# Keys of a gated linear attention turned head by head in half of the array's rows, two units ahead, with f and k loaded a step sooner

## The chip, the cores and the metric

The kernel runs on one core of a Trainium2 chip. The metric is the device time of one execution in microseconds. The engines are named as in the profile: PE (TensorE, matrix products; PEld is its weight load), DVE (VectorE), ACT (ScalarE), POOL (GpSimd) and SP (SyncE, which here issues transfers).

## What is computed

Two parts, one behind the other, all in FP32: a recurrence with a state per head, and a bilinear feed-forward layer.

```python
# q, k, v, f_logit: (4, 8, 768, 48); w_a, w_b: (384, 1536); w_out: (1536, 384)
f = 1.0 / (1.0 + np.exp(-f_logit))
for t in range(S):
    state = f[:, :, t, :, None] * state + np.einsum('bhd,bhe->bhde', k[:, :, t], v[:, :, t])
    y[:, :, t] = np.einsum('bhd,bhde->bhe', q[:, :, t], state)
x = y.transpose(0, 2, 1, 3).reshape(B * S, H * D)      # 3072 x 384
return ((x @ w_a) * (x @ w_b)) @ w_out
```

## The kernel before, in words

**Units and blocks.** The recurrence is cut into 16 units: a batch, half of its tokens (384) and four heads. In a unit's tiles two heads lie one above the other, in rows 0 to 47 and 64 to 111, and two such pairs side by side (`n`). Tokens go in chunks of 128 (`c`) and sub-chunks of 64 (`p`). Two units fill a block: 384 tokens of x with all 384 columns. There are eight blocks.

**The steps of a unit** (all in `by_quotients`):
- `loads_of` (line 209): transfers of f, k, q (two each, one for each half of the rows) and v on the SP queue, into one of three sets of tiles, so that a unit's loads wait until the unit three before has done with them.
- `front_parts` (line 302): ACT makes sigmoid(f) and its opposite, POOL an affine step; DVE scans f (L322), takes reciprocals (L330), scans the inverse (six of L335), multiplies k by the inverse and q by the products of f (L339).
- `scores` (L392): 24 products of k with q, 64 tokens each, in quarters of the array, into the bank pair ps_x.
- `mask` (L405): DVE reads ps_x and writes the masked scores to `at`.
- `turn` (L416): six transposes of 128 x 128, each of one chunk of one pair of heads, all 128 rows at once, into ps_x, over the scores that the mask has read. `turned` (L425) copies them to kT on ACT.
- `gains` (L440): products of kT and v for each sub-chunk, into ps_x over the transposes; `carry` (L467, L469) adds them to the states on DVE, and `hand_on` (L478) scales the last state for the other half of the tokens.
- `within` (L489) and `across` (L515): products of `at` with v and of the states with q, both into ps_y; `out_of_bank` (L534) copies ps_y out with three copies on ACT, and `stores_of` (L554) moves it into the block's xT with five small transfers on SP.

**The layer.** Blocks 0 and 1 go through plain products (`up`, L598; `product`, L620 on DVE). For blocks 2 to 7 `up_triples` (from line 714, products at L720) computes both factors with 15 products in place of 18; it works on sums of weights (`combine_w_ba`, L633 and, where DVE makes them, L1262) and of x (`combine_x`, L704), in four quarters `j` of 15 steps each. ACT copies (L1307 through a planner's line) and DVE adds (L712) take the results out of four banks, ps_f. `down` (products at L822) multiplies by w_out for pairs of token groups, with seven products in place of eight; DVE and ACT add up (L837 to L857), and SP stores rows of the result (L861).

**What sets the order of work.** The first four units and the first products are written out by hand. From there on a list `main` holds the layer's steps, and a planner (line 1168 on) lays the remaining work between them: `Line` objects hold steps with an engine, a planned cost and marks that they need, and `fill` emits the first step of any line that fits: for PE when its inputs are planned to be there, for other engines when `delays` finds that no step of `main` would come late by it. `emit_until` forces what a block must have before it starts. There are six lines, tried in this order:

```python
for_out, for_x, core, fore, loads, for_ba = lines = [Line() for _ in range(6)]
```

`core` holds `core_parts(s)` (line 901) for s = 4 to 16, strictly in order: within of unit s-1 and scores of s; mask; turn; turned; gains of s and across of s-1; carries; hand-on; copies out and stores of s-1. `fore` holds the fronts, `loads` the transfers of unit s, which wait for the stores of unit s-3. A unit's scores wait for its whole front. PE visits a unit three times: within and scores, turn, gains and across.

Of the kernel before, what the change touches and what calls it, by code (L numbers as in the profile page):

```python
# [12 lines left out]
FP32 = mybir.dt.float32  # L13
# [7 lines left out]
C = 128  # L21
FINE = (0, 1, 2, 4, 8, 16)
BLK = 384
# [3 lines left out]
R = 64  # L27
# [115 lines left out]
def by_quotients(ctx, tc, q, k, f_logit, v, moe_w_a, moe_w_b, moe_w_out, out, ident, weights, bad, ps_f):  # L143
    nc = tc.nc
    B, H, D, S = q.shape
# [4 lines left out]
    NQ = H // 4  # L150
    NC = BLK // C
# [3 lines left out]
    NU = B * NH * NQ  # L155
    NBLK = B * NH
    NSET = 3
# [3 lines left out]
    sb1 = ctx.enter_context(tc.tile_pool(name="sb1", bufs=1))  # L161
# [8 lines left out]
    sets = []  # L170
    for i in range(NSET):
        t = {n: fixed([128, 2, BLK], f"{n}_in{i}") for n in "qkf"}
# [120 lines left out]
    PE, DVE, ACT, POOL, SP = range(5)  # L293
    live = {}
# [4 lines left out]
    def halves(x):  # L299
        return x.rearrange("p n s -> p (n s)")  # L300
# [55 lines left out]
    ps_x, ps_y = (ps_a.tile([128, 2, 512], FP32, tag=n, name=n) for n in ("ps_x", "ps_y"))  # L356
# [23 lines left out]
    def pair_of(x):  # L380

        return [x[:, i] for i in range(2)]
# [17 lines left out]
    def mask(u):  # L400
# [4 lines left out]
        nc.vector.tensor_tensor(to, x, tri.broadcast_to((128, 2, 2 * NC, SUB)), ALU.mult)  # L405
        live[u]["at"] = at

    def turn(u):

        kf = halves(sets[u % NSET]["k"])  # L410
        live.setdefault(u, {})["kT"] = sb1.tile([128, 2, NC, 128], FP32, tag="kT", name="kT")
        ps = live[u]["turned"] = [ps_f[idle.pop(0)] for _ in range(2)] if u in FIRST else pair_of(away(u))
        for n in range(2):
            for c in range(NC):
                o = n * BLK + c * C
                nc.tensor.transpose(ps[n][:, c * C:c * C + C], kf[:, o:o + C], ident)  # L416
# [10 lines left out]
    def gains(u, chunks=range(NC)):  # L427

        _, half, _ = unit(u)
        t, kT = sets[u % NSET], live[u]["kT"]  # L430
        last = half == NH - 1
        ps = live[u]["turned"]
        for n in range(2):
            for c in chunks:
                for p in range(2):
                    if last and c == NC - 1 and p == 1:
                        continue
                    for h in range(2):
                        r = slice(SUB * p, SUB * p + SUB)
                        nc.tensor.matmul(  # L440
                            ps[p][R * h:R * h + D, (n * NC + c) * D:(n * NC + c) * D + D],
                            lhsT=kT[r, n, c, R * h:R * h + D],
                            rhs=t["v"][r, n, c, h * D:h * D + D],
                            start=True,
                            stop=True,
                        )
# [126 lines left out]
    ISSUE = 430  # L573
# [327 lines left out]
    def core_parts(s):  # L901


        u = s - 1
        if u < 2 * NQ:
            yield PE, 1000, 0, scores, s
        elif s < NU:
            yield PE, 1600, 0, within_and_scores, u
        else:
            yield PE, 1000, 20 * BEAT, within, u  # L910
        if s < NU:
            yield DVE, 880, 0, mask, s
            yield PE, 850, 0, turn, s
            yield ACT, 700, 0, turned, s
        if u < 2 * NQ:
            yield PE, 1000, 0, gains, s
        elif s < NU:
            yield PE, 1550, 0, gains_and_across, u
        else:
            yield PE, 1000, 0, across, u  # L920
        if s < NU:
            for j in range(NJ - 1 if unit(s)[1] == NH - 1 else NJ):
                yield DVE, 180, 0, carry, s, j
            if unit(s)[1] < NH - 1:
                yield DVE, 320, 0, hand_on, s
        if u >= 2 * NQ:
            for part in range(3):
                yield ACT, 490, 0, out_of_bank, u, part
            begin, *stores = stores_of(u)
            yield SP, 0, 0, begin  # L930
            for do in stores:
                yield SP, ISSUE, 5000, do

    def within_and_scores(u):
        within(u)
# [1 line left out]

    def gains_and_across(u):
        gains(u + 1)
        across(u)  # L940

    some = fixed([128, 2], "some")

# [30 lines left out]
    with tc.manual_schedule():  # L974
# [161 lines left out]


        w_out_sums, (w_before, w_over) = list(combine_w_out()), combine_w_ba()
        main, beside, behind, ending = [], {}, {}, []
        for blk, i in ups[alone:]:  # L1140
            main.extend(up_steps(blk, i))
            main.append(on(DVE, 480, 2, product))
# [2 lines left out]
        for blk in range(NBLK):  # L1145
            if blk >= 2:
                beside[len(main)] = "x", blk
                main.extend(up_triples(blk))
                behind[blk] = len(main)
                ahead = 16  # L1150
            b, odd = divmod(blk, 2)
            pairs = (((blk - 1, 0), (blk, 0)), ((blk, 1), (blk, 2))) if odd else (((blk, 1), (blk, 2)),)
            if blk == 1:
                pairs = (((0, 1), (0, 2)), *pairs)
            for two in pairs if blk else ():
                beside.setdefault(len(main), "out")
                first, *steps = down(two, ending if blk == NBLK - 1 and two is pairs[-1] else None)
                at = len(main) - ahead
                main.insert(at, first)
                beside = {n + (n > at): x for n, x in beside.items()}  # L1160
                if blk == NBLK - 1 and two is pairs[0]:
                    steps.insert(0, on(DVE, 700, 0, sum_held))
                    steps.append(on(PE, 100, 0, check_held))
                main.extend(steps)
                behind.setdefault("down", len(main))
                ahead = 10
# [11 lines left out]
                    needs, past = (), 0  # L1178
                return self, len(self.steps)

        for_out, for_x, core, fore, loads, for_ba = lines = [Line() for _ in range(6)]
        marks = {"out": for_out.extend(w_out_sums)}
        for_ba.extend(w_before)
        marks["ba"] = for_ba.extend(w_over, past=behind[1])
        stores = {}
        for s in range(2 * NQ, NU + 1):
            if s < NU:
                loaded = ()
                if s - NSET in stores:
                    at = stores[s - NSET]  # L1190
                    loaded = (loads.extend([(SP, ISSUE, 6000, do) for do in loads_of(s)], needs=(at,)),)
                ready = fore.extend(
                    [(e, load, 0, *do) for part in front_parts(s) for e, load, *do in part], needs=loaded
                )
            for step in core_parts(s):
                blk, second = divmod(s - 1, NQ)
                core.extend(
                    (step,),
                    needs=(ready,) if step[3] in (scores, within_and_scores) else (),
                    past=behind[blk - 2] if step[3] in (across, gains_and_across) and not second else 0,  # L1200
                )
            if s > 2 * NQ:
                stores[s - 1] = core, len(core.steps)
# [88 lines left out]
        for done, (engine, load, due, do, *args) in enumerate(main):  # L1292
# [8 lines left out]
            else:  # L1301
                ready = max(now, last_copy if engine >= COPIED else 0) + LATENCY
# [357 lines left out]
```

## Time and profile before

| | us |
|---|---|
| median of 3 runs | 597.28 (597.1 to 597.85) |
| the profiled execution: its own time | 596.37 |
| its span | 594.6 |
| DVE, ACT, POOL busy | 412.2, 268.7, 77.7 |
| PE idle after 130 us of the span, in all | 2.3 |

What the stages are, by the time in the span: up to 50 us loads, first units and the conversion of the first weights; 50 to 139 plain products of blocks 0 and 1; 139 to 192 the first down phases; from 192 on block after block (2 to 7) a product phase and a down phase. Units 4 to 15 pass through between 128 and 467 us. The last two blocks have no attention work beside them.

Some groups by shape, for the steps that the change concerns (columns: line, engine, operation, names, shapes, count; busy us, mean ns; idle before):

```profile
L416 PE MATMUL ps_x<-ident,k_in 128*128 128x128 f32 x78 | 10.6, 273 | 0.0
L440 PE MATMUL ps_x<-v_in,kT 64*48 64x48 f32 x568 | 10.0, 209 | 0.5 <-issue 0.5
L425 ACT COPY kT<-ps_x 128x768 f32<-128x768 f32 x13 | 10.4, 798 | 44.5 <-PE ps_x L416 43.7 <-DVE sums L712 0.8
```

A matmul's mean is its length from first input to last output; matmuls follow one another at shorter distance, so their cost to the stream is read from start to start. An FP32 product stands in the trace as two records, a transpose as one. The page counts PE as idle only where no matmul is in flight, so short stops between records don't show as idle.

### The profile page before, as it was taken

How to read it: one execution, taken by the hardware profiler on the slowest of the kernel's cores; microseconds unless marked ns; L12 is line 12 of the kernel's file. 1: busy time of each engine (PE TensorE's matmuls, PEld its weight loads, DVE VectorE, ACT ScalarE, POOL GpSimd, SP SyncE). 2: the span in 40 equal slices, each digit the busy share in tenths (PEclk: the TensorE clock that was granted, in tenths of full speed). 3: DMA queues.
4: the chain of work that ended last, by engine and by line, in shares of the span. 5: the costliest groups of instructions: out<-in, count | busy, mean ns of one | idle time of the engine just before them, and what ended most of it. 6: DMA issues, size and time to landing. Idle time of an engine off the chain costs nothing.

```text
span 594.6 us, 13952 instructions
## 1 busy us (share of the span) xinstructions
PE 572.6 (96%) x5802; PEld 512.9 (86%) x5802; DVE 412.2 (69%) x786; ACT 268.7 (45%) x507; POOL 77.7 (13%) x71
## 2 busy tenths in 40 slices
PE   2899999999999999999999999999999999999997
PEld 1655655557999999999999999999999999999996
DVE  6899545599978678958894678847785165836751
ACT  6589959753132464245521444326431345135300
POOL 6254425355000000000000000000000000000000
PEclk9899999999999999999999999999999999999999
DMA  9696699089542440044004410041001100000001
GB/s 211 183 267 197 213 273 268 0 147 186 116 141 71 115 93 10 15 120 95 2 1 125 108 23 2 2 105 43 3 1 47 48 1 0 2 28 1 0 29 33
DMA packets 33561, 49.43 MB, mean 83 GB/s; under 512 B 3984, under 2 KB 25264, under 8 KB 33488
## 3 DMA queue, kind: packets, MB, share of 16 engines
q1 hardware_dynamic: 30000, 42.19, 25.5%
q0 software_dynamic: 3056, 5.92, 5.9%
q8 instruction: 47, 0.77, 0.5%
q10 hardware_dynamic: 432, 0.34, 0.2%
q14 instruction: 26, 0.21, 0.1%
HBM read 33.23 MB, written 4.72 MB: 64 GB/s over the span
## 4 chain that ended last, share of the span: by engine, by line
PE 85%; DVE 10%; issue 2%; ACT 1%; DMA 1%; SPq 0%; DVEq 0%; ACTq 0%
PE ps_f L720 35%; PE ps_f L822 28%; PE ps_f L598 13%; PE ps_y L489 2%; DVE inv L335 2%; PE ps_y L515 2%; PE ps_x L392 2%; PE ps_x L440 1%; PE ps_x L416 1%; DVE sums L712 1%; DVE groups L712 1%; DVE spare L335 1%; DVE q_in L339 1%; DVE f_in L322 1%; DVE w_ba L73 1%
## 5 line engine op out<-in xcount | busy, mean ns | idle before, releaser
L598 PE MATMUL ps_f<-xT,w_ba 128*128 128x384 f32 x288 | 95.6, 489 | 1.5 <-DMA xT<-y 1.4
L1307 ACT COPY sums<-ps_f 128x384 f32<-128x384 f32 x120 | 57.4, 480 | 75.9 <-PE ps_f L720 68.2
L598 PEld LDWEIGHTS ps_f<-xT,w_ba 128*128 128x128 f32 x288 | 53.8, 190 | 38.2 <-issue 2.2
L1307 ACT COPY groups<-ps_f 128x384 f32<-128x384 f32 x120 | 57.7, 481 | 62.9 <-PE ps_f L720 39.9
L720 PE MATMUL ps_f<-xT,w_ba 128*128 128x192 f32 x384 | 78.4, 327 | 0.0
L720 PEld LDWEIGHTS ps_f<-xT,w_ba 128*128 128x128 f32 x384 | 64.7, 190 | 0.2
L720 PE MATMUL ps_f<-groups,w_ba 128*128 128x192 f32 x288 | 55.5, 327 | 0.0
L720 PE MATMUL ps_f<-x_sums,raw 128*128 128x192 f32 x288 | 54.1, 331 | 1.2 <-DVE groups L712 0.9
L822 PE MATMUL ps_f<-w_out,sums 128*128 128x192 f32 x288 | 52.2, 329 | 0.3 <-DVE groups L620 0.3
L822 PE MATMUL ps_f<-w_out,groups 128*128 128x192 f32 x288 | 51.7, 328 | 0.0
L720 PEld LDWEIGHTS ps_f<-x_sums,raw 128*128 128x128 f32 x288 | 46.9, 190 | 4.3 <-DVE groups L712 1.8
L822 PE MATMUL ps_f<-spare,sums 128*128 128x192 f32 x288 | 49.0, 326 | 0.0
L720 PEld LDWEIGHTS ps_f<-groups,w_ba 128*128 128x128 f32 x288 | 47.8, 190 | 0.5 <-ACT groups L1307 0.3
L822 PEld LDWEIGHTS ps_f<-w_out,sums 128*128 128x128 f32 x288 | 47.1, 190 | 1.3 <-DVE groups L620 0.6
L318 POOL TENSOR_SCALAR inv<-inv 128x768 f32<-128x768 f32 x14 | 13.1, 935 | 266.7 <-ACT inv L315 266.7
L822 PEld LDWEIGHTS ps_f<-w_out,groups 128*128 128x128 f32 x288 | 47.1, 190 | 0.7
L822 PEld LDWEIGHTS ps_f<-spare,sums 128*128 128x128 f32 x288 | 47.1, 190 | 0.1
L60 POOL TENSOR_SCALAR sums<-sums 128x768 f32<-128x768 f32 (+1 forms) x20 | 40.4, 2018 | 43.9 <-ACT sums L58 43.8
L712 DVE TENSOR_TENSOR sums<-sums,groups 128x768 f32<-128x768 f32 x36 | 34.7, 965 | 14.2 <-ACT groups L1307 13.7
L712 DVE TENSOR_TENSOR sums<-ps_f,sums 128x384 f32<-128x384 f32 x60 | 32.8, 553 | 16.5 <-PE ps_f L720 15.0
L720 PE MATMUL ps_f<-x_sums,w_ba 128*128 128x192 f32 x192 | 39.3, 327 | 0.5 <-DVE sums L712 0.5
L720 PE MATMUL ps_f<-xT,raw 128*128 128x192 f32 x192 | 39.4, 328 | 0.0
(142 smaller groups left out, 869.3 us busy)
## 6 DMA issues: line engine op xcount, KB each, us to landing
raw<-w_ba POOLq DMA_DIRECT2D x11, 512.0 KB, 8.6
k_in<-in_k_dram SPq DMA_DIRECT2D x32, 144.0 KB, 4.2
q_in<-in_q_dram SPq DMA_DIRECT2D x32, 144.0 KB, 4.4
v_in<-in_v_dram SPq DMA_DIRECT2D x16, 288.0 KB, 5.0
raw<-in_moe_w_out_dram SPq DMA_DIRECT2D x6, 768.0 KB, 5.9
out_dram<-o SPq DMA_DIRECT2D x22, 192.0 KB, 1.9
f_in<-in_f_logit_dram SPq DMA_DIRECT2D x28, 144.0 KB, 3.0
xT<-y SPq DMA_DIRECT2D x45, 72.0 KB, 2.2
```

Source lines behind the costliest of these rows:

```text
L60: nc.gpsimd.tensor_scalar(h, h, HI_MAX, None, ALU.min)
L73: nc.vector.tensor_tensor(dst[:, rows], hu[:, rows], bit[:, rows], ALU.add)
L318: nc.gpsimd.tensor_scalar(inv, inv, EXP_K, 1.0, ALU.mult, ALU.add)
L335: nc.vector.tensor_tensor_scan(inv[:, w], inv[:, w], none[:, 0:C], first, ALU.mult, ALU.add)
L392: nc.tensor.matmul(ps[h][SUB * p:SUB * p + SUB, o:o + SUB], lhsT=kf[r, tokens(n, c, p)], rhs=qf[r, tokens(n, c, p)], start=True, stop=True,)
L489: nc.tensor.matmul(ps[p][e:e + D, o:o + SUB], lhsT=t["v"][r, n, c, h * D:h * D + D], rhs=at[r, h, o:o + SUB], start=o == 0, stop=True, ski ...
L515: nc.tensor.matmul(ps[p][e:e + D, o:o + SUB], lhsT=st[j][r, n], rhs=qf[r, tokens(n, c, p)], start=False, stop=True, skip_group_check=True,)
L598: nc.tensor.matmul(ps[nm][:, 0:BLK], lhsT=w[:, kt, ft * 128:ft * 128 + 128], rhs=xT[blk][:, kt], start=kt == 0, stop=kt == NKT - 1,)
L712: nc.vector.tensor_tensor(to, x, y, op)
L720: nc.tensor.matmul(ps[:, g], lhsT=sums_of_w[name][:, g, 128 * j:128 * j + 128], rhs=sums_of_x[blk][name], start=start and g == 0, stop=Tru ...
L822: nc.tensor.matmul(to, lhsT=x[:, i // 2, i % 2], rhs=w[:, NI * (i % 2) + i // 2], start=start and i == 0, stop=i == HFT - 1, skip_group_ch ...
L1307: do(*args)
```

## The change

- `turn` is kept for units 0 to 3. From unit 4 on `turn_heads` makes twelve transposes in place of six: for each chunk and pair, the upper and the lower head by itself, 48 rows in, 48 columns out, into bank h of a pair.
- From unit 8 (`AHEAD`) on these transposes stand in the step of `gains_and_across` two units earlier, behind `across`. They go to columns of ps_x behind the gains (four chunks) and of ps_y behind the outputs (two chunks), and `turned_heads` copies them with two copies of 384 and 192 columns. For units 4 to 7 they stay where `turn` stood, and one copy of 576 columns takes them out.
- kT lies head by head, 48 columns each without gaps; `gains` reads it through `keys`.
- Copies out, stores, the q product of the front, and the last sums of w_b and w_a get lines of their own. The front without its q product waits for f and k, and gains (from unit 8 on) wait for it; scores wait for the q product.
- f and k of a unit are loaded when unit s-3 has handed its state on; q and v as before behind its stores.

The order of instructions that results: 72 transposes of 128 columns are replaced by 144 of 48, thirteen copies to kT of 768 columns by one of 768, four of 576, and eight each of 384 and 192; on DVE, POOL and SP the same instructions stand in another order.

```diff
+    AHEAD = 4 * NQ
+    NX = 4
+    turns = [(n * NC + c, n, c) for n in range(2) for c in range(NC)]
+    def turn_heads(u):
+        kf = halves(sets[u % NSET]["k"])
...
+        live[u]["turned"] = pair_of(ps_x)
+        for i, n, c in turns:
+            ps, o = (ps_x, 2 * NC * D + i * D) if i < NX else (ps_y, BLK + (i - NX) * D)
+            if u < AHEAD:
+                ps, o = ps_x, i * D
+            for h in range(2):
+                r, at = slice(R * h, R * h + D), n * BLK + c * C
+                nc.tensor.transpose(ps[:, h, o:o + D], kf[r, at:at + C], ident[r, R * h:R * h + D])
...
+        if u < AHEAD:
+            copy(0, ps_x, 0)
+        else:
+            copy(0, ps_x, 2 * NC * D)
+            copy(NX, ps_y, BLK)
...
-                            lhsT=kT[r, n, c, R * h:R * h + D],
+                            lhsT=kT[r, h, n * NC + c],
...
-            yield PE, 850, 0, turn, s
-            yield ACT, 700, 0, turned, s
-        if u < 2 * NQ:
-            yield PE, 1000, 0, gains, s
-        elif s < NU:
-            yield PE, 1550, 0, gains_and_across, u
+        if s < min(NU, AHEAD):
+            yield PE, 600, 0, turn_heads, s
+            yield ACT, 650, 0, turned_heads, s
+        if s < NU:
+            yield PE, 1200 if u < 2 * NQ else 1850, 0, gains_and_across, u
...
+        if AHEAD <= u + 2 < NU:
+            yield ACT, 850, 0, turned_heads, u + 2
...
     def gains_and_across(u):
         gains(u + 1)
-        across(u)
+        if u >= 2 * NQ:
+            across(u)
+        if AHEAD <= u + 2 < NU:
+            turn_heads(u + 2)
...
-        for_out, for_x, core, fore, loads, for_ba = lines = [Line() for _ in range(6)]
+        for_out, for_x, outs, away_to, core, late, over, fore, loads, for_ba = lines = [Line() for _ in range(10)]
...
-        for_ba.extend(w_before)
-        marks["ba"] = for_ba.extend(w_over, past=behind[1])
+        marks["ba"] = over.extend(w_over, (for_ba.extend(w_before),), past=max(behind[1], begins[2] - 50))
...
+        def load(s, names, behind_it):
+            if s - NSET not in behind_it:
+                return ()
+            past = max(0, begins.get(s // NQ - 2, 0) - 40)
+            return (loads.extend([(SP, ISSUE, 6000, do) for do in loads_of(s, names)], (behind_it[s - NSET],), past),)
+        def factors_of(s):
+            if s < NU:
+                steps = [(e, load, 0, *do) for part in front_parts(s) for e, load, *do in part]
+                ready["k", s] = fore.extend(steps[:-1], load(s, "fk", handed))
+                last_step[s] = steps[-1]
+            if 2 * NQ <= s - 1 < NU:
+                ready["q", s - 1] = late.extend([last_step[s - 1]], (ready["k", s - 1], *load(s - 1, "qv", stores)))
...
+            factors_of(s + 1)
             for step in core_parts(s):
...
+                needs = {
+                    turn_heads: ("k", s), scores: ("q", s), within_and_scores: ("q", s), gains_and_across: ("k", s + 1)
+                }.get(step[3] if step[3] is not gains_and_across or s + 1 >= AHEAD else None)
...
+                if outs.steps and step[3] in (within, within_and_scores):
+                    needs = (*needs, (outs, len(outs.steps)))
...
+                if step[3] in (carry, hand_on):
+                    handed[s] = mark
```

More of the change, by code (lines that the diff above doesn't have):

```diff
@@ L406, in mask, with keys, turned_heads, copy @@
         live[u]["at"] = at
+    AHEAD = 4 * NQ
[3 more added lines that the diff above has]
+        kf = halves(sets[u % NSET]["k"])
+        live.setdefault(u, {})["kT"] = sb1.tile([128, 2, NC, 128], FP32, tag="kT", name="kT")
+        live[u]["turned"] = pair_of(ps_x)
[6 more added lines that the diff above has]
+                nc.tensor.transpose(ps[:, h, o:o + D], kf[r, at:at + C], ident[r, R * h:R * h + D])
+    def keys(u):
+        kT = live[u]["kT"]
+        if u < 2 * NQ:
+            return kT.rearrange("s n c (h d) -> s h (n c) d", h=2)[:, :, :, 0:D]
+        return kT.rearrange("s n c x -> s (n c x)")[:, 0:4 * NC * D].rearrange("s (h i d) -> s h i d", h=2, d=D)
+    def turned_heads(u):
+        def copy(first, ps, o):
+            n = min(2 * NC - first, NX if u >= AHEAD else 2 * NC)
+            nc.scalar.copy(
+                keys(u)[:, :, first:first + n], ps[:, :, o:o + n * D].rearrange("s h (i d) -> s h i d", d=D)
+            )
+        if u < AHEAD:
[3 more added lines that the diff above has]
+            copy(NX, ps_y, BLK)
     def turn(u):
@@ L429, in gains @@
         _, half, _ = unit(u)
-        t, kT = sets[u % NSET], live[u]["kT"]
+        t, kT = sets[u % NSET], keys(u)
         last = half == NH - 1
@@ L925, in core_parts, with out_parts @@
                 yield DVE, 320, 0, hand_on, s
+    def out_parts(u):
         if u >= 2 * NQ:
@@ L928, in core_parts, with store_parts @@
                 yield ACT, 490, 0, out_of_bank, u, part
[L929 to L932, printed above, removed]
+        if AHEAD <= u + 2 < NU:
+            yield ACT, 850, 0, turned_heads, u + 2
+    def store_parts(u):
+        begin, *stores = stores_of(u)
+        yield SP, 0, 0, begin
+        for do in stores:
+            yield SP, ISSUE, 5000, do
     def within_and_scores(u):
@@ L1138, in by_quotients @@
         w_out_sums, (w_before, w_over) = list(combine_w_out()), combine_w_ba()
-        main, beside, behind, ending = [], {}, {}, []
+        main, beside, begins, behind, ending = [], {}, {}, {}, []
         for blk, i in ups[alone:]:
@@ L1147, in by_quotients @@
                 beside[len(main)] = "x", blk
+                begins[blk] = len(main)
                 main.extend(up_triples(blk))
@@ L1185, in by_quotients @@
         stores = {}
-        for s in range(2 * NQ, NU + 1):
[L1187 to L1194, printed above, removed]
+        handed, ready = {}, {}
@@ L1195, in by_quotients @@
+        last_step = {}
+        factors_of(2 * NQ)
+        for s in range(2 * NQ, NU + 1):
+            factors_of(s + 1)
             for step in core_parts(s):
                 blk, second = divmod(s - 1, NQ)
-                core.extend(
+                needs = {
+                    turn_heads: ("k", s), scores: ("q", s), within_and_scores: ("q", s), gains_and_across: ("k", s + 1)
+                }.get(step[3] if step[3] is not gains_and_across or s + 1 >= AHEAD else None)
+                needs = (ready[needs],) if needs in ready else ()
+                if outs.steps and step[3] in (within, within_and_scores):
+                    needs = (*needs, (outs, len(outs.steps)))
+                mark = core.extend(
@@ L1198, in by_quotients @@
                     (step,),
-                    needs=(ready,) if step[3] in (scores, within_and_scores) else (),
+                    needs=needs,
                     past=behind[blk - 2] if step[3] in (across, gains_and_across) and not second else 0,
                 )
-            if s > 2 * NQ:
-                stores[s - 1] = core, len(core.steps)
+                if step[3] in (carry, hand_on):
+                    handed[s] = mark
+                if step[3] in (across, gains_and_across):
+                    copied = outs.extend(out_parts(s - 1), (mark, *([stores[s - 2]] if s - 2 in stores else [])))
+                    if s > 2 * NQ:
+                        stores[s - 1] = away_to.extend(store_parts(s - 1), (copied,))
```

## The prediction, made before the changed kernel was run

> **What bounds the kernel now.** I read the page's busy line and its slices first, then the chain of work that ended last, then TensorE's timeline around the steps that the change touches.
>
> ```profile
> PE 572.6 (96%) x5802; PEld 512.9 (86%) x5802; DVE 412.2 (69%) x786; ACT 268.7 (45%) x507; POOL 77.7 (13%) x71
> PE   2899999999999999999999999999999999999997
> PE 85%; DVE 10%; issue 2%; ACT 1%; DMA 1%; SPq 0%; DVEq 0%; ACTq 0%
> ```
>
> TensorE (PE) is busy in all slices but the first two, and holds 85% of the chain. So time is won only by fewer TensorE microseconds, or by ending the short stops inside its stream. The stream around unit 7's turn (columns: start us, duration, engine, line, what, count):
>
> ```profile
> 185.56 2.11 PE L822 MATMUL ps_f<-spare,groups 128*128 128x192 f32 x12
> 187.60 0.89 PE L489 MATMUL ps_y<-at,v_in 64*48 64x64 f32 x48
> 188.31 0.92 PE L392 MATMUL ps_x<-q_in,k_in 48*64 48x64 f32 x48
> 189.16 2.22 PE L822 MATMUL ps_f<-w_out,sums 128*128 128x192 f32 x12
> 191.21 0.82 PE L416 MATMUL ps_x<-ident,k_in 128*128 128x128 f32 x6
> 191.87 0.82 PE L720 MATMUL ps_f<-x_sums,raw 128*128 128x192 f32 x4
> 192.52 0.81 PE L720 MATMUL ps_f<-x_sums,w_ba 128*128 128x192 f32 x4
> 193.26 0.69 PE L440 MATMUL ps_x<-v_in,kT 64*48 64x48 f32 x37
> ```
>
> A row's duration includes the last matmul's own length, so I read costs from start to start. Four records of 128x192 take 0.65 (191.87 to 192.52), 163 ns each, 0.85 ns a column. The turn (L416, six of 128 columns) takes 191.21 to 191.87, 0.66 us, 110 ns each, the same pace, with nothing lost on either side. The steps on small pieces of the array lose at their edges: the 12 records at 185.56 need 12 x 0.163 = 1.96 and the next row starts after 2.04 (0.08 lost); L489 and L392 are 96 records of 64 columns, four at a time in four quarters, 96 x 64 x 0.85 / 4 = 1.31, and they take 1.56 (0.25 lost); the next 12 records take 2.05 (0.09 lost). About 0.4 per visit to the small pieces.
>
> The stops, in the same timeline:
>
> ```profile
> 225.89 2.11 PE L720 MATMUL ps_f<-x_sums,raw 128*128 128x192 f32 x12
> 228.46 0.92 PE L720 MATMUL ps_f<-x_sums,w_ba 128*128 128x192 f32 x4 [0.46 <-DVE sums L712]
> 299.93 0.81 PE L720 MATMUL ps_f<-xT,w_ba 128*128 128x192 f32 x4
> 301.60 1.57 PE L720 MATMUL ps_f<-x_sums,raw 128*128 128x192 f32 x8 [0.86 <-DVE groups L712]
> ```
>
> From 225.89 to 228.46 twelve records needed 1.96 and took 2.57: 0.61 lost. From 299.93 to 301.60 four needed 0.65 and took 1.67: 1.02 lost. Both wait for VectorE's sums (L712), which free the banks, and VectorE is late because scans and products of the next unit (L322, L335, L339) lie between them: on its timeline they take 4.5 of the 6.7 us from 221.14 to 227.86. Counted in this way, five such stops cost 2.5 us: 0.61 at 225.89 in block 2, 0.23 at 290.33 and 1.02 at 299.93 in block 3, 0.39 at 346.67 and 0.27 at 356.35 in block 4.
>
> **What the skill says of these steps.** The Trainium skill, TensorEngine Tiling (Array Packing), Key Properties: changing the tiling mode drains TensorE. The trace agrees, with about 0.4 us per visit as above, and the forecast takes that number. TensorE: Matmul & The Clock Gate, section LDWEIGHTS: a load takes columns / 1.2 GHz, and the row count doesn't matter. For the new turn this is the key rule: 48 rows are loaded no faster than 128. By the page 128 columns cost 107 ns, an estimate. The trace before can't confirm it for transposes: their loads are shorter in the record than those of the matmuls.
>
> ```profile
> L720 PEld LDWEIGHTS ps_f<-xT,w_ba 128*128 128x128 f32 x384 | 64.7, 190 | 0.2
> L392 PEld LDWEIGHTS ps_x<-q_in,k_in 48*64 48x64 f32 x672 | 11.7, 134 | 1.0 <-DVE q_in L339 0.7 <-DVE w_ba L73 0.2 <-issue 0.2
> L416 PEld LDWEIGHTS ps_x<-ident,k_in 128*128 128x128 f32 x78 | 9.3, 141 | 0.9 <-issue 0.4
> ```
>
> From 64 to 128 columns a matmul's load grows by 56 ns (0.87 a column), which leaves a fixed 78; a transpose's 141 less 78 is 63 ns for 128 columns. I go by 63, from the trace, and keep 107 as the upper end of a load.
>
> **The change, part by part.**
>
> *The turn itself.* For units 4 to 15, six transposes of 128 columns become twelve of 48, alternately in the upper and the lower half of the rows. Removed: 12 x 0.66 = 7.9 us. Added: if the halves work side by side, six rounds. A round isn't shorter than 48 x 0.85 = 41 ns nor longer than the load at 107, so a turn is 0.25 to 0.64 us; with 63 ns it is 0.38. That pieces with the same columns and other rows do overlap is shown by L392 and L489, whose pace needs all four quarters at once. If the halves take turns instead, it is 12 x 63 = 0.76, or 12 x 107 = 1.28 at the worst.
>
> *Where it stands.* In the new order of instructions the turns of units 8 to 15 follow the products with states directly, so they share that visit; only one more change of mode, to half-rows, is paid (0.06 is seen between L489 and L392, which change no size; up to 0.25; I take 0.1). Eight times (0.38 + 0.1 - 0.66) = -1.4 us. The turns of units 4 to 7 stay alone between full matmuls, and where the old turn lost nothing at its edges, the new one pays a visit, about 0.35: four times (0.38 + 0.35 - 0.66) = +0.3 us.
>
> *Copies to kT.* Before, 798 ns for 768 columns, and 482 for 384: 0.82 ns a column and 0.17 fixed. After, one of 576 columns (0.64) for units 4 to 7, one of 384 and one of 192 (0.48 + 0.32) for the others: per unit the same or less. ScalarE is busy 45%, so nothing on the path. The copy has to end before the next scores overwrite the bank, as before.
>
> *The chain of a unit.* Turn, copy and gains stood one behind the other after the mask; now the keys are turned a unit ahead, and gains wait only for the mask. Nobody on the path waited for the copy (the largest kT wait is ScalarE's own, for the turn), so alone it is worth nothing. It does let a unit begin sooner.
>
> *f and k a step sooner.* The load of f and k (two transfers each, 3.0 and 4.2 us to landing) waits for the states' hand-on instead of the stores, and the k part of the front no longer waits for q. On VectorE this puts a unit's scans earlier. In the new order of instructions, third and fourth quarter of blocks 2 and 3 and all but the first quarter of block 4 hold no scan between the sums, only a q product in block 2; before, each stop had scans ahead of it. The first quarter of block 4 keeps five scans and a k product, so the 0.39 at 346.67 may stay. VectorE does the same work, and by the windows it is busy 47 to 49 us in each 60 from 142 to 320, so part of the lateness comes back where the scans now lie, in the down phases and first quarters. Of 2.5 I keep two thirds: -1.7 us. On the SP queue, output stores now go behind loads of q and v in places; what is delayed so is the reuse of the output tile, one down phase (13.7 us) later, with 1.9 us to landing: nothing.
>
> *The sums of w_b and w_a* (four of 1.22 us on VectorE, from 142 to 163 us before) move behind other steps, the last of them to just ahead of block 2's first products, which need them. Counted at nothing: VectorE is idle for 9.5 of the 58 us from 142 to 200. If that doesn't cover the last one, it costs up to 1.2 us.
>
> Sum: -1.4 + 0.3 - 1.7 = **-2.8 us**. The profiled execution is 596.37 us (span 594.6) and would become 593.6; the median is 0.9 above it, 597.28, and becomes **594.5**.
>
> **The rivals.** About 0.2%, 1.2 us, is what a measurement can tell from no change.
>
> *Slow small transposes (slower).* The half-row transposes don't overlap, or each pays its load. With twelve turns at zero the sum is 8 x (0.1 - 0.66) + 4 x (0.35 - 0.66) - 1.7 = -7.4 us, so a turn of 0.62 us breaks even and one of 0.72 is measurably slower. Halfway from 0.38 to the worst, 0.83: 12 x 0.83 - 7.4 = +2.6, **599.9**. For it: a load longer than its matmul, as here (63 to 107 against 41 ns), is nowhere in this trace. Against: the four quarters overlap.
>
> *VectorE's lateness only moves (no change).* The stops come back in the down phases or at the start of block 2, where the four w sums and x sums crowd: -1.1 for the turns and +0.8 for a new stop there, **597.0**. For it: VectorE is 80% busy. Against: the emission holds back steps that would delay a main step.
>
> *Both good.* A turn takes 0.27, the added change of mode is hidden, and all five stops go: 8 x (0.27 - 0.66) + 4 x (0.27 + 0.3 - 0.66) - 2.5 = -6.0, **591.3**.
>
> That the change isn't done is no rival: the order of instructions has 144 transposes of 48 columns in place of 72 of 128.
>
> **How the numbers follow.** Forecast 594.5, chance 0.44; both good 0.14; no change 0.22; slow transposes 0.20. Hence faster 0.58, same 0.22, slower 0.20. The range goes from 591.0 (both good) to 601.0, past the middle of the slow case; what is above it (turns over 0.93 us) I give 1 in 10, what is below 1 in 20. The likeliest case's own range is 593 to 596.
>
> **What would show it.** Right: a turn's row for units 8 to 15 that takes 0.3 to 0.5 us from start to start; for 4 to 7 0.05 to 0.1 before and 0.2 after it; no wait above 0.3 for L712 in the later quarters of blocks 2 and 3; TensorE's idle after 130 us (2.3 us in the page's sense) under 1. Wrong: turn rows above 0.65 us, or new waits of TensorE for L712, L405 or L1307 in the down phases.

## The result, and the profile after

The changed kernel is slower: median 600.56 us of 8 runs (598.58 to 601.95), against 597.15 of the kernel before on the same chip; the ratio is 1.0055, with an interval of 1.0041 to 1.0070. Its profiled execution took 598.58 us (span 596.7), 2.2 more than that of before. It ran at the full TensorE clock, while five of the eight runs had a mean clock of 0.991 to 0.994 and took 600.4 to 602.0, for a reason that no run here shows; so the trace shows 2.2 of the 3.4 us between the medians.

The lines of the page that answer to those of before, TensorE's busy time and the chain of work that ended last:

```profile
PE 571.0 (96%) x5874; PEld 508.7 (85%) x5874; DVE 411.1 (69%) x786; ACT 267.7 (45%) x515; POOL 78.5 (13%) x71
PE 79%; DVE 11%; DMA 4%; issue 3%; POOL 1%; ACT 1%; SPq 1%; DVEq 0%; ACTq 0%
```

TensorE is busy 1.6 us less than before, as a shorter turn would have it, and the kernel is longer all the same: the chain runs over TensorE for 79% instead of 85%, and DMA, 1% before, holds 4%. Something off TensorE holds it up. Its timeline shows where (start, duration, line, count; in the changed kernel L862 is the product with w_out that was L822, L425 the new turn, L752 the sums that were L712):

```profile
151.48 3.52 PE L862 MATMUL ps_f<-spare,sums 128*128 128x192 f32 x20
158.04 2.22 PE L862 MATMUL ps_f<-spare,groups 128*128 128x192 f32 x12 [3.04 <-DVE u L891]
160.46 1.73 PE L862 MATMUL ps_f<-w_out,sums 128*128 128x192 f32 x9 [0.21 <-DVE o L897]
```

Twenty records need 20 x 0.163 = 3.26 us; the next row starts 6.56 after them. So 3.30 us are lost in one place, in the first down phase, where nothing was lost before. VectorE is what TensorE waits for, but VectorE itself stood still there for 5.13 us, waiting for POOL:

```profile
153.34 0.42 DVE L335 TENSOR_TENSOR_SCAN inv<-inv,zero 128x128 f32<-128x128 f32 x1 [5.13 <-POOL inv L318]
```

Unit 6's inverse scan (L335) is next in VectorE's order, and the affine step (L318) that feeds it hadn't run; in the kernel before this scan began at 148.74. Behind it on VectorE stand the carries and the sum L891 that frees a bank for TensorE. So POOL's timeline has to be read. In the kernel before (L630 issues the accumulating transfers that add up the weights in `raw`, 512 KB each):

```profile
130.80 0.82 POOL L318 TENSOR_SCALAR inv<-inv 128x768 f32<-128x768 f32 x1 [5.04 <-ACT inv L315]
131.68 6.16 POOL L630 DMA_DIRECT2D raw<-w_ba  x5
143.12 1.20 POOL L630 DMA_DIRECT2D raw<-w_ba  x1 [5.29 <-DMA raw<-w_ba]
145.84 1.20 POOL L630 DMA_DIRECT2D raw<-w_ba  x1 [1.52 <-DMA raw<-w_ba]
147.13 1.57 POOL L318 TENSOR_SCALAR inv<-inv 128x768 f32<-128x768 f32 x1
```

In the changed kernel (L670 is that line now):

```profile
130.88 0.82 POOL L318 TENSOR_SCALAR inv<-inv 128x768 f32<-128x768 f32 x1 [7.83 <-ACT inv L315]
131.76 7.39 POOL L670 DMA_DIRECT2D raw<-w_ba  x6
147.26 1.20 POOL L670 DMA_DIRECT2D raw<-w_ba  x1 [8.11 <-DMA raw<-w_ba]
151.20 1.20 POOL L670 DMA_DIRECT2D raw<-w_ba  x1 [2.73 <-DMA raw<-w_ba]
152.48 0.82 POOL L318 TENSOR_SCALAR inv<-inv 128x768 f32<-128x768 f32 x1
```

In both, unit 6's affine step stands behind the last two transfers, and these wait for earlier ones to land, since they add to the same tile. ACT had its input ready at 142.7 in both. Two things differ. One transfer more stands behind the affine step of 130.8 (the order is three, affine, eight instead of four, affine, seven). And the last waits are longer, because SP now moves f and k of unit 7 beside them:

```profile
138.80 1.90 SPq L217 DMA_DIRECT2D f_in<-in_f_logit_dram  x2
140.79 2.62 SPq L217 DMA_DIRECT2D k_in<-in_k_dram  x2
```

Before, these four were issued from 161.63 and from 162.64 on. While they run, POOL's last two issues stand 3.9 us apart (147.26 and 151.20), where they stood 2.7 apart before (143.12 and 145.84). In the chain of work the transfer issued at 134.70, the fifth of six in a row, is now a link of 16.2 us; most of that is the queue of transfers ahead of it, since in a run below, without the loads beside it, the same one takes 13.9 from issue to landing.

To compare traces without their different first 139 us (that point lies between 137.8 and 139.7 in all profiles), I use the time from the first product with w_out to the end of the last one, the **layer stretch**: 450.9 us before, 453.8 after. A "stop" is what the distance between two rows of the layer's own products, with nothing of the recurrence between them, has beyond 163 ns a record (326 for 384 columns), where it is over 0.12. The 2.9 us by which the stretch grew are made up of:

| | us |
|---|---|
| turns of units 8 to 15 | -1.3 |
| turns of units 5 to 7 (unit 4's stands before the stretch) | +0.15 |
| the stop in the first down phase | +3.30 |
| a stop right after it (158.04 to 160.46) | +0.47 |
| a stop at 184, behind a sum of w_a and w_b | +0.52 |
| stops from 195 us on, the larger of them for sums: 3.9 before, 4.0 after | +0.1 |
| the rest, spread over small gaps and edges | -0.3 |

### The profile page after: what moved, and what is told of

Its sections match the earlier page's. It is cut to its first block, busy times and chain, and to the rows that moved or that the text cites. A ratio compares the mean times of both kernels' runs of the same rounds, so it can differ in the third digit from the quotient of the medians.

```text
span 596.7 us, 14141 instructions
## 1 busy us (share of the span) xinstructions
PE 571.0 (96%) x5874; PEld 508.7 (85%) x5874; DVE 411.1 (69%) x786; ACT 267.7 (45%) x515; POOL 78.5 (13%) x71
## 4 chain that ended last, share of the span: by engine, by line
PE 79%; DVE 11%; DMA 4%; issue 3%; POOL 1%; ACT 1%; SPq 1%; DVEq 0%; ACTq 0%
PE ps_f L760 38%; PE ps_f L862 23%; PE ps_f L638 11%; DMA raw<-w_ba 3%; PE ps_y L529 2%; PE ps_y L555 1%; PE ps_x L392 1%; PE ps_x L480 1%; DVE inv L335 1%; DVE f_in L322 1%; DVE st L509 1%; DVE spare L335 1%; DVE q_in L339 1%; DVE sums L752 1%; PE ps_x L425 1%
## 5 line engine op out<-in xcount | busy, mean ns | idle before, releaser
L862 PE MATMUL ps_f<-w_out,sums 128*128 128x192 f32 x288 | 51.9, 329 | 0.5 <-DVE groups L660 0.3
L862 PE MATMUL ps_f<-w_out,groups 128*128 128x192 f32 x288 | 52.1, 329 | 0.0
L862 PE MATMUL ps_f<-spare,sums 128*128 128x192 f32 x288 | 50.5, 329 | 0.4 <-DVE sums L752 0.4
L862 PEld LDWEIGHTS ps_f<-w_out,sums 128*128 128x128 f32 x288 | 47.2, 190 | 1.4 <-DVE groups L660 0.6
L862 PEld LDWEIGHTS ps_f<-spare,sums 128*128 128x128 f32 x288 | 46.9, 190 | 1.1 <-DVE sums L752 0.7
L862 PEld LDWEIGHTS ps_f<-w_out,groups 128*128 128x128 f32 x288 | 47.2, 190 | 0.7
L752 DVE TENSOR_TENSOR sums<-sums,groups 128x768 f32<-128x768 f32 x36 | 34.4, 954 | 19.4 <-ACT groups L1379 19.0
L318 POOL TENSOR_SCALAR inv<-inv 128x768 f32<-128x768 f32 x14 | 14.1, 1008 | 253.9 <-ACT inv L315 253.8
L752 DVE TENSOR_TENSOR sums<-ps_f,sums 128x384 f32<-128x384 f32 x60 | 32.7, 553 | 15.7 <-PE ps_f L760 13.9
```

The lines of the kernel that those rows point to most:

```text
L318: nc.gpsimd.tensor_scalar(inv, inv, EXP_K, 1.0, ALU.mult, ALU.add)
L752: nc.vector.tensor_tensor(to, x, y, op)
L862: nc.tensor.matmul(to, lhsT=x[:, i // 2, i % 2], rhs=w[:, NI * (i % 2) + i // 2], start=start and i == 0, stop=i == HFT - 1, skip_group_ch ...
```

## The experiments

All were compared with the kernel before on the same chip, and ratios are to it. Not all ran on one chip, so between experiments the ratios and the layer stretches are to be compared rather than the times. Line numbers shift a little from kernel to kernel (the sums are L752 to L758).

**Unit 6's affine step on VectorE.** The theory: the wait comes through POOL's queue. Rival: VectorE would be late there anyway, through its own order.

```diff
-            nc.gpsimd.tensor_scalar(inv, inv, EXP_K, 1.0, ALU.mult, ALU.add)
+            eng = nc.vector if u == 6 else nc.gpsimd
+            eng.tensor_scalar(inv, inv, EXP_K, 1.0, ALU.mult, ALU.add)
```

> The changed kernel, with one instruction moved: unit 6's affine step (L318) runs on VectorE instead of POOL; all else stands in the same order. My theory (the POOL queue): TensorE's stop of 3.3 us at 151 us comes from this step, which waited in POOL's queue behind two issues of weight sums; so the stop goes, and the two smaller ones behind it (0.3 at 158, 0.5 at 184) as well: about 4 us less than the changed kernel's fast profile, 594.5 to 595.5, faster than the kernel before by 0.3 to 0.4%. Rival (VectorE would be late there anyway, through the order of its steps): a stop of 2 us or more stays near 151 to 158, and the time stays at 598 to 601.

Measured: 595.99 us, ratio 0.9986 (0.9977 to 0.9996), layer stretch 450.1. The stop of 3.30 is gone, and so is the one behind it:

```profile
150.38 3.52 PE L863 MATMUL ps_f<-spare,sums 128*128 128x192 f32 x20
153.73 2.11 PE L863 MATMUL ps_f<-spare,groups 128*128 128x192 f32 x12
```

POOL's last two transfers are as late as in the changed kernel (issued at 146.03 and 149.91), but TensorE doesn't stop for them. The stop of 0.5 us behind a sum of w_a and w_b stays (0.53 at 179), which I had not expected, and the gain on the kernel before is half of what I had expected. One instruction on another engine is worth 3.7 us of the layer stretch, and the change without this stop is a little faster than the kernel before.

**f and k of unit 7 loaded late.**

```diff
-                ready["k", s] = fore.extend(steps[:-1], load(s, "fk", handed))
+                ready["k", s] = fore.extend(steps[:-1], load(s, "fk", stores if s == 7 else handed))
```

> The changed kernel, with the load of f and k of unit 7 alone back behind unit 4's stores; POOL's order is unchanged. If the weight sums landed late because this load shared the DMA engines with them (4 of the 5.4 us by which the last of them is issued late), they are issued at about 147 instead of 151 us, and the stop at 151 is under 0.5 us; time 595 to 596. If it is the order on POOL alone (one sum more between two affine steps), the stop stays at 2 us or more and the time at 598 to 601.

Measured: 597.43, ratio 1.0015 (1.0002 to 1.0029), layer stretch 451.1. POOL's last two issues are 2.7 us apart again, and unit 6's affine step follows them:

```profile
148.38 1.20 POOL L670 DMA_DIRECT2D raw<-w_ba  x1 [1.53 <-DMA raw<-w_ba]
149.66 0.82 POOL L318 TENSOR_SCALAR inv<-inv 128x768 f32<-128x768 f32 x1
```

Counted from the first product with w_out, the affine step starts at 7.9 us in the kernel before, 10.5 here, and 12.8 in the changed kernel. So of its 4.9 us of lateness 2.3 come from unit 7's load beside the sums and 2.6 from the order on POOL. A stop of 0.87 stays, where I had expected 0.5 at most, and the time is above the 595 to 596 that I had expected: the load is some 2.4 of the 3.3.

**Both together.** If POOL's queue is the only way in which the early load costs, the two must not add up.

```diff
+            eng = nc.vector if u == 6 else nc.gpsimd
...
+                ready["k", s] = fore.extend(steps[:-1], load(s, "fk", stores if s == 7 else handed))
```

> Unit 6's affine step on VectorE and f and k of unit 7 loaded behind the stores, together. The first alone measured 595.99, the second 597.43, the changed kernel 600.56. Theory (both act through POOL's queue ahead of unit 6's affine step, nothing else): with the affine step out of that queue the early load costs nothing, so both together are 595.5 to 596.5, the first alone. Rival (the early load also costs by itself, through the transfers of weights or VectorE's order): 594.5 to 595.3.

Measured: 596.20, ratio 0.9994 (0.9986 to 1.0003), layer stretch 450.0 against 450.1 for the affine step alone. They don't add up: with the affine step out of that queue, the early load costs nothing that these runs can tell.

**All f and k loaded late.** This tests the prediction's claim that the early loads buy little.

```diff
-                ready["k", s] = fore.extend(steps[:-1], load(s, "fk", handed))
+                ready["k", s] = fore.extend(steps[:-1], load(s, "fk", stores))
```

> The changed kernel, with the loads of f and k of all units back behind the stores. By my theory the stop at 151 goes as in the run with unit 7 alone. The early loads of the other units bought nothing (the stops for L712's sums are 3.1 us in both kernels), so the time is within 0.5 us of that run, 595 to 596.5. Rival: the early loads do clear stops in the blocks, and without them this kernel is 1 to 2 us slower than the one with unit 7 alone.

Measured: 635.94, ratio 1.0648 (1.0624 to 1.0673). My expectation was far off. In this kernel TensorE's longest wait is for VectorE, and VectorE's own wait behind it is for the blocks' inputs (us in total, times, longest):

```profile
PE ps_f L760 <- DVE x_sums L744: 23.9, 5, 7.2
```

```profile
DVE x_sums L744 <- DMA xT<-y: 20.3, 3, 7.0
```

The blocks' inputs come late: units are not finished when the layer needs their tokens. In the changed line-up gains of a unit wait, in the same step as the products with states of the unit before, for keys turned two units ahead. Loaded late, k holds back the unit before it as well. Read so, the early load isn't a bonus of the new place of the turn but its price. That the blocks' inputs come late is shown; that this order is the reason is read from the code and wasn't tested by itself.

**The half-row transposes alone, at the old place.** The kernel before, with `turn_heads` and its single copy for units 4 to 15 where `turn` stood and nothing else.

```diff
+    AHEAD = 1 << 10
...
-            yield PE, 850, 0, turn, s
-            yield ACT, 700, 0, turned, s
+            yield PE, 850, 0, turn_heads, s
+            yield ACT, 700, 0, turned_heads, s
```

> The kernel before, with the turn of units 4 to 15 head by head in half the rows, at its old place; the order of instructions is the same. From the changed kernel's rows for units 4 to 7, where a turn takes 0.50 instead of 0.66 us and loses 0.2 at its edges, each turn costs 0.05 more: +0.6 us over 12, no difference that can be measured (597 to 598.5). If the half rows were worth something by themselves, 0.16 a turn, it would be -1.9 us (595.3).

Measured: 596.85, ratio 1.0006 (0.9992 to 1.0019), layer stretch 451.1 against 450.9. As expected, worth nothing by themselves.

**Two other forms of the turn.** For the stream, a turn behind the products with states takes 0.50 us in the changed kernel (first row to the product after it):

```profile
198.98 0.45 PE L425 MATMUL ps_x<-ident,k_in 48*128 48x48 f32 x8
199.26 0.29 PE L425 MATMUL ps_y<-ident,k_in 48*128 48x48 f32 x4
199.48 0.92 PE L760 MATMUL ps_f<-x_sums,w_ba 128*128 128x192 f32 x4
```

That is 12 x 41 ns, which two readings explain.

```diff
+        if u < AHEAD:
+            for i, n, c in turns:
+                for h in range(2):
+                    r, at = slice(R * h, R * h + R), n * BLK + c * C
+                    nc.tensor.transpose(ps_x[:, h, i * R:i * R + R], kf[r, at:at + C], ident[r, R * h:R * h + R])
+            return
+        for h in range(2):
+            for i, n, c in turns:
...
```

> The changed kernel's turn rows show 12 transposes of 48 columns in 0.50 us, 41 ns each: two readings. Stream: the halves don't overlap, each transpose takes its 48 columns x 0.85 ns. Pairs: the two halves overlap, and a pair is paced at 82 ns by something else (a load). Here the turns of units 4 to 7 use 64 columns in place of 48, and those of units 8 to 15 do all six of the upper half, then all six of the lower. Stream: 64 columns give 12 x 54 = 0.65 us of rows; upper-then-lower stays 0.50. Pairs: 64 columns stay at 0.50; upper-then-lower rises to 12 x 82 = 0.98. The time as a whole moves by less than 1 us from the changed kernel in the stream reading and by up to +4 us in the pairs reading.

Measured in a single run, too few for a comparison of times: 597.77, layer stretch 454.9, 1.1 more than the changed kernel's. 64 columns take 0.52 (131.74 to 132.26), as the pairs reading said. Upper-then-lower takes 0.66 (218.34 to 219.00), between the two.

Single starts settle it. In the changed kernel's turn at 220.2 the records start two at a time, an upper and a lower one, 3 to 5 ns apart: at 220.23, .33, .39, .46, .52 and .58. The halves do overlap; the first round takes 0.10, each later one 0.06, and of the last 0.15 to the next product some 0.09 is the edge. With 64 columns the later rounds take 0.06 as well (131.74, .85, .91, .98, 132.04, .10). So the pace is neither the stream nor 82 ns a pair, but about 60 ns a pair, for 48 columns as for 64; "82" came from spreading the edges over the rounds. With all upper ones first, the first lower one starts 0.17 after the first upper one, so only part of the two halves overlaps.

**Shorter scans on VectorE.** The prediction's second term was the stops for sums, put down to scans ahead of them. The base is the kernel with unit 6's affine step on VectorE; its stops from 195 us on add up to 4.0.

```diff
+            m = 16 if u >= AHEAD else C
+            w = slice(w.start, w.start + m)
-            nc.vector.tensor_tensor_scan(inv[:, w], inv[:, w], none[:, 0:C], first, ALU.mult, ALU.add)
+            nc.vector.tensor_tensor_scan(inv[:, w], inv[:, w], none[:, 0:m], first, ALU.mult, ALU.add)
```

> On top of the kernel with unit 6's affine step on VectorE (596.0). Units 8 to 15: each of the six inverse scans reads and writes 16 of its 128 columns (the rest of the scan is left out), at the same place in the order, so that VectorE gets about 6 x 0.3 = 1.8 us per unit back. Theory (the stops for L752's sums in blocks 2 to 4, about 3 us, come from fronts on VectorE ahead of them): they fall under 1.5 us, and the kernel gains 1 to 2 us, 594 to 595. Rival (the stops come from the sums' own chain of copies, products and sums, whatever is in front): stops within 0.5 us of the 3, time 595.5 to 596.5.

Measured: 595.68, ratio 0.9987 (0.9979 to 0.9995), against 0.9986 for its base; stops 4.1 in all, where the base has 4.0. VectorE's scans did become shorter, by some 11 us in all (a scan of 16 columns takes 0.17 to 0.23 us, one of 128 takes 0.40 to 0.47), but the stops of 0.45, 0.59 and 0.42 us in blocks 3, 4 and 5 are unchanged to within 0.01. My theory of scans falls. The timeline of this kernel around the one in block 4:

```profile
341.61 0.26 DVE L510 COPY st<-ps_x 128x96 f32<-128x96 f32 x1 [1.56 <-PE ps_x L428]
341.91 1.41 DVE L512 TENSOR_TENSOR st<-st,ps_x 128x96 f32<-128x96 f32 x5
...
343.03 0.81 PE L763 MATMUL ps_f<-xT,w_ba 128*128 128x192 f32 x4
343.35 0.40 DVE L521 TENSOR_SCALAR st<-st,f_in 128x48 f32<-128x48 f32 x2
343.66 1.02 DVE L755 TENSOR_TENSOR sums<-ps_f,sums 128x384 f32<-128x384 f32 x2
344.27 0.92 PE L763 MATMUL ps_f<-x_sums,raw 128*128 128x192 f32 x4 [0.43 <-DVE sums L755]
```

VectorE had been idle for 1.56 us. Then six carries and two hand-ons, 2.05 us, stand ahead of the two sums that TensorE needs. The planner counts a carry at 180 ns; the row has 1.41 / 5 = 282, of which 253 is the mean of one instruction and the rest lies between them.

**Carries counted at 290 ns.** On the same base.

```diff
-                yield DVE, 180, 0, carry, s, j
+                yield DVE, 290, 0, carry, s, j
```

> On top of the kernel with unit 6's affine step on VectorE (595.99): the planner counts 290 ns for a carry in place of 180; the trace has 282. Theory (what is left of the stops in the first quarters, 0.4 to 0.6 us each in blocks 3, 4 and 5, comes from seven or eight instructions of the carries, 2.1 us, that the planner lets in ahead of two sums because it counts them too low): those stops fall below 0.25 us each and the kernel comes to 594.8 to 595.5. Rival (the stops come with the order of TensorE's own steps, or come back elsewhere): 595.6 to 596.8.

Measured: 594.76, ratio 0.9968 (0.9958 to 0.9979), layer stretch 448.7 against 450.1. At the same place the sums now stand between the carries, and the row of TensorE that waited follows without a gap (its four records start at 342.78 and need 0.65):

```profile
341.65 0.83 DVE L510 TENSOR_TENSOR st<-st,ps_x 128x96 f32<-128x96 f32 x3
342.40 0.55 DVE L753 TENSOR_TENSOR sums<-ps_f,sums 128x384 f32<-128x384 f32 x1
342.78 0.81 PE L761 MATMUL ps_f<-xT,w_ba 128*128 128x192 f32 x4
...
343.43 1.14 PE L761 MATMUL ps_f<-x_sums,raw 128*128 128x192 f32 x6
```

The stops in blocks 3 and 4 are gone and the one of 0.42 in block 5 stays; in block 2 new ones of 0.42 and 0.74 appear. The expectation holds for two of the three places, and the time is just below its range. But the stops from 195 us on fall only from 4.0 to 3.6. Of the 1.4 us of layer stretch, 0.8 lie before that, where I had not looked for them: a stop of 0.45 at the start of the stretch is gone, and the one of 0.53 at 179 is 0.16. The same number moved other steps too.

**The same number in the kernel before.**

```diff
-                yield DVE, 180, 0, carry, s, j
+                yield DVE, 290, 0, carry, s, j
```

> The kernel before with one number changed: the planner counts 290 ns for a carry in place of 180. It asks whether the 1.2 us that this brought on top of the changed kernel with the affine step on VectorE (594.76 against 595.99) belongs to the changed line-up. If it is worth the same in any line-up: 594.9 to 595.7 here, and the turn behind the products with states is worth only some 0.5 us. If it belongs to the changed line-up, where the carries came to stand ahead of two sums at the start of blocks 3 to 5 (the kernel before has no stop there): 596.0 to 597.5.

Measured: 596.20 against 596.80, ratio 0.9986 (0.9976 to 0.9996), but the layer stretch is 450.7 against 450.9. The time lies in the second range as it was written, but with a gain of 0.14% where the second reading expects none and the first 0.2 to 0.3%. It doesn't settle how much of the 1.2 us belongs to the changed line-up.

**Products of units 8 to 15 on POOL.** Again on the kernel with unit 6's affine step on VectorE.

```diff
-            [(DVE, 880, times, "k", inv), (DVE, 880, times, "q", F)],
+        by, cost = (POOL, 1800) if u >= AHEAD else (DVE, 880)
...
+            [(by, cost, times, "k", inv), (by, cost, times, "q", F)],
...
+            eng = nc.gpsimd if u >= AHEAD else nc.vector
+            eng.tensor_tensor(halves(t[nm]), halves(t[nm]), by, ALU.mult)
```

> On top of the kernel with unit 6's affine step on VectorE (596.0). For units 8 to 15 the products of k with the inverse and of q with the products of f go from VectorE (0.95 us each) to POOL, which is idle after 190 us. Theory (VectorE's lateness makes the stops for L752's sums): stops fall by half or more, 594.5 to 595.5. Rival (POOL takes several us for each product, or slows VectorE's own instructions while it runs, so that the keys come late or the sums take longer): no gain or a loss, 596 to 600, with VectorE's mean for a 768-column sum above 955 ns or new stops for k_in or q_in.

Measured: 594.76, ratio 0.9962 (0.9948 to 0.9976), layer stretch 449.1; stops from 195 us on 2.6 instead of 4.0, a third less and not half. A product takes 1.82 on POOL in thirteen of the sixteen cases and 2.4 to 2.5 in the others, 0.95 on VectorE.

**The order of that kernel, with the products back on VectorE.** Instruction for instruction the same order; only the engine of sixteen products differs.

```diff
-            eng = nc.gpsimd if u >= AHEAD else nc.vector
+            eng = nc.vector
```

> The order of instructions of the kernel with the products on POOL (594.76), with those sixteen products back on VectorE at their places. If the order brought the gain (carries and sums interleaved): 594.5 to 595.3. If VectorE's freed time did (16 x 0.95 us): stops return at the places where a product now stands, 595.6 to 597, the time of the kernel with the affine step alone or worse.

Measured: 596.65, ratio 1.0005 (0.9996 to 1.0015), layer stretch 450.7, stops 3.5. So the order alone brings nothing. Freed time alone didn't either: the shorter scans took some 11 us off VectorE in the old order and left the time where it was, while the products on POOL take 16 x 0.95 = 15 us off it. The gain needs VectorE's time in those places together with the order planned for it.

**Carries counted at 290 ns and the products on POOL.**

```diff
-                yield DVE, 180, 0, carry, s, j
+                yield DVE, 290, 0, carry, s, j
```

> Carries counted at 290 ns and the products of units 8 to 15 on POOL, together. Theory (carries' cost): a little below the products alone (594.76), 594.0 to 594.6. Rival (the order changes, nothing is left to win there): 594.6 to 596.

Measured: 596.14, ratio 0.9990 (0.9979 to 1.0000), layer stretch 450.1. The gains don't add up, as the rival had it, and the time is above even its range. Two stops of 1.48 and 1.25 are new in block 2. At the first of them, POOL and VectorE:

```profile
214.38 1.82 POOL L341 TENSOR_TENSOR k_in<-k_in,inv 128x768 f32<-128x768 f32 x1 [14.59 <-issue]
214.61 2.40 DVE L755 TENSOR_TENSOR groups<-groups,sums 128x768 f32<-128x768 f32 x1
```

This sum takes 0.95 elsewhere. It began just after a product on POOL and ended 0.81 after that one's end, almost as if it had started only then. The second stop is for a sum that stands behind another such: it began at 234.01, 0.6 us into a product on POOL, took 2.57 and ended 0.81 after that product. That the first stop follows from the long sum is read from its place; TensorE waits there for ScalarE.

## Why the prediction was wrong, by its own steps

*The turn itself, and where it stands: right.* Forecast 8 x (0.38 + 0.1 - 0.66) = -1.4, measured 8 x (0.50 - 0.66) = -1.3. The rounds of 63 ns, taken from the difference of two load rows, measured 60 and stand for the choice between two sources: by the Trainium skill (TensorE: Matmul & The Clock Gate, section LDWEIGHTS) a load of 128 columns would have been 107, an estimate, and turns would have come to 0.64. That a load sets the 60 is not shown, so the nearness of 63 may be chance. That the rows of a load don't matter, its rule there, agrees with the runs in so far as 48 and 64 rows have the same pace; but there the columns of the result differ too. Units 4 to 7: forecast +0.07 each, measured +0.05 (unit 4: 131.54 to 135.67 is 4.13 where it was 4.08). The first rival, slow small transposes, is out.

*Copies and the chain of a unit: right.* No wait of TensorE for kT appears.

*Sums of w_b and w_a on VectorE: mis-sized.* Counted at nothing, with 1.2 as the bound; the third of the four, at 183.40, stands ahead of two sums and costs 0.52.

*Stops for the sums, -1.7: wrong.* All stops from 195 us on total 3.9 before and 4.0 after. Of those that I had named, the 1.02 in block 3 is gone, as are 0.23 and 0.27, and of the 0.61 in block 2 0.28 is left; but the 0.39 at 347 became 0.59, and 0.45 (270) and 0.42 twice (407, 420) are new. This is the second rival, lateness that only moves. Its cause was named wrongly too: with seven eighths of the inverse scans' elements left out, the stops in blocks 3 to 5 stay. Carries, planned at 180 ns and taking 282 each with their gaps, stand ahead of the sum at the stop in block 4; changing this number removed two of the stops. Taking the products off VectorE in a new order shortened the stops by a third.

*"On the SP queue ... nothing": the step that failed.* It asked what the earlier loads would delay on SP's own queue. It did not ask what the transfers would run beside, nor walk POOL's queue, whose order it had: eleven transfers, of which the later ones wait for earlier ones to land, and unit 6's affine step behind the last of them. The prediction moved the sums of w_b and w_a as four instructions on VectorE, without the POOL half of the same chain. That step was worth +3.3 us, and +0.5 right behind it, and it turned a gain into a loss: without it the gain is 0.14%, against a forecast of 2.8 us or 0.5%, and what is still missing is mostly the stops for the sums above. Both halves of the cause are shown: without the affine step in that queue the kernel is at 0.9986, without the load beside it at 1.0015, with neither at 0.9994, against 1.0055. That the time still lies inside the range, near its upper end, is luck: the range reached so far up for slow turns, and no rival had this mechanism. None of the signs of being wrong named it either; they looked for waits on other lines.

The rule behind it stands in the Trainium skill (TensorE: Matmul & The Clock Gate, section "Architectural detail: the array is 16× 32×32, not 1× 128×128"): each core of GpSimd takes its queue strictly first in, first out. The trace agrees: 0.82 us of arithmetic, whose input was ready at 142.7, stood until 152.48 behind two issues.

## What to carry to other kernels

When a load or a step moves, walk every in-order queue between its old and its new place, and those of the engines that it doesn't issue on: look for an instruction that waits for a landing, and ask what stands behind it and who waits for that. A small step on a path of inputs (here 0.8 us of affine arithmetic) doesn't belong behind transfers that wait for one another. And where a planner orders instructions, compare its costs with the rows of the trace before blaming the engine: one number, 180 for 282 ns, was worth about as much here (1.2 us on top of the changed line-up, though only some 0.6 in the kernel before) as the new place of all eight turns (1.3, read from their rows).

Two versions beat both kernels most clearly: the changed one with unit 6's affine step on VectorE and carries counted at 290 ns (ratio 0.9968, 0.9958 to 0.9979), or with the products of units 8 to 15 on POOL instead of the latter (0.9962, 0.9948 to 0.9976). Together they don't.

## What the runs showed of the hardware

- Two transposes in the two halves of the rows, issued alternately, run at the same time: 60 ns a pair, for 48 and for 64 columns. Issued half by half, twelve take 0.66 instead of 0.50 us.
- Accumulating transfers of 512 KB inside SBUF, queued one behind another, let the next issue that waits for them go every 2.7 us (143.12 to 145.84 before, 145.64 to 148.38 with unit 7's load late), and every 3.9 with 576 KB of other loads beside them (147.26 to 151.20).
- A VectorE sum of two SBUF tiles that begins during a POOL product of two SBUF tiles took 2.40 us instead of 0.95. The Trainium skill (SBUF — State Buffer, section Who interferes with whom) states this: with two inputs in SBUF it contends with a GpSimd instruction that reads SBUF, and the later one is blocked until the other has finished. The row agrees, with 0.23 us between the starts. In the two kernels with products on POOL eight sums of 768 columns began during one, and each ended 0.81 us after it; sums that read a bank of PSUM began during one as well and took 0.55 to 0.56, as elsewhere. It is the price of the products on POOL, which pay all the same in the kernel in which only three such sums meet them.
